# Position bias of an attention kernel: the activity tests on float16 whole distances, two of three on ScalarE, and the first sum out of PSUM in one VectorE instruction

## The chip, the core and the metric

The kernel runs on one core of a Trainium2 chip. Its five engines work side by side: TensorE (PE; its weight loads are PEld), VectorE (DVE), ScalarE (ACT), GpSimd (POOL) and SyncE (SP), which issues most of the DMAs. The metric is the time of one execution on the device in microseconds, lower is better.

## The reference

Attention with a learned position bias, then a three-way max block, then eight experts mixed by a doubly normalised gate. This case touches the position bias only:

```python
rel = (pos[:, None] - pos[None, :]).astype(np.float32)
psi_rel = np.log1p(np.abs(rel))
psi_i = np.log1p(np.maximum(pos[:, None].astype(np.float32), 1.0))
x = (psi_rel / psi_i)[..., None]
h = np.maximum(x @ w1 + b1, 0.0)      # 32 hidden units
bias = h @ w2                          # 8 heads
scores = scores + bias.transpose(2, 0, 1)[None, :, :, :]
```

There are 2 batches, 8 heads, 576 positions and a head width of 64. For a row i and a hidden unit d, the unit is active at column j where w1·log1p|i−j| + b1·log1p(i) is positive. The bias of a head is then a sum, over the active units, of w1·w2 (multiplied by log1p|i−j| / log1p(i)) and of b1·w2.

## The kernel before

The program has four stages one after the other: the position bias, which is written to a DRAM tensor `bias_d`; the attention of 8 heads; the max block; the experts. Each engine runs its instructions in the order in which the Python code issues them; nothing reorders them. An engine that waits holds up everything behind it in its own order.

The bias stage works in 36 steps (`g16`) of 16 rows i. A step needs four activity tiles (`gen_s(g)`, 144 in all), each [128, 576] in float16: 4 rows i times 32 hidden units on the partitions, 576 columns j along the row. They come from a table `lw` of float32 logarithms (L213, loaded in two parts and multiplied by w1 on ScalarE, L239): a test tile is a window of it, shifted by 4 columns from one `g` to the next. VectorE compares the window with a threshold (L282, giving +0.5 or −0.5) for 12 of every 20 tiles (`ON_DVE`), ScalarE takes the Sign of the window plus a bias (L280, giving +1 or −1) for the rest. The tiles lie in a pool of 12, three steps deep.

`bias_mm` (L323) multiplies each tile with 32-column weights on TensorE, in two float16 parts and two column halves, for two sums: `ps[0]` (A, to be multiplied by the logarithm) and `ps[1]` (B). That is 32 products a step. As the tests are ±, a constant has to be added: for B by two more products with `cb` (L332), for A by the bias of ScalarE's instruction.

`bias_ev` takes A out of PSUM: ScalarE scales it and adds the constant (L339), GpSimd multiplies the result by the table `l16` (L342, VectorE in the last two steps). `bias_out` (L347) takes B out of PSUM on VectorE, scales it and adds the first tile; the result `bo` goes to DRAM through SP's queue. VectorE's order within a step is: `gen_s` for the step after next, then `bo`. Two PSUM buffers for each sum let TensorE be one step ahead.

GpSimd also prepares the operands of the attention's first two heads (`prep_head`, by L61 for a copy that rounds, and L190 for the rest that the copy leaves): head 0 in 18 instructions, one after every second step, then head 1 in 12. Head 1's inputs are loaded in three parts in steps 9, 15 and 18.

Before the first test there is a chain on VectorE that makes the weights `wb` (L244 to L272). It starts when the parameters `par` have landed.

Of the kernel before, what the change touches and what calls it, by code (L numbers as in the profile page):

```python
# [27 lines left out]
SH = S // 2  # L28
# [22 lines left out]
def make_body(stop=None):  # L51
    def body(tc, a):
# [21 lines left out]
        with ctx, tc.manual_schedule():  # L74
# [16 lines left out]
            def prep_w64(r, hi, lo):  # L91
                """A float64 weight tile [128, 512], made float32 on its bits and split, in steps."""
# [4 lines left out]
                # the exponent's floor is where float32's lowest exponent, and so 0, is made  # L97
# [25 lines left out]
            def w_step(n=1, last=99):  # L123
                """The next n steps of the weights' preparation, up to an item."""
# [15 lines left out]
            # ------------------------------------------------ operands of the heads  # L140
# [25 lines left out]
            def prep_head(h, k, part=None):  # L166
                """Operands of head h, piece k: hi, then what is left."""
# [34 lines left out]
            # ------------------------------------------------ position bias  # L202
            with ExitStack() as bctx:
# [9 lines left out]
                cuts = (0, 476, L4_W)  # L213
                nc.scalar.dma_start(out=lw[:, cuts[1]:], in_=a["tab4"][:, cuts[1]:])
                dma(lw[:, :cuts[1]], a["tab4"][:, :cuts[1]])
# [5 lines left out]
                # products that nobody reads, to have the tensor engine's clock up when the data are there  # L221
# [6 lines left out]
                half = bc.tile([32, 96], F32, name="half")  # L228
                G.memset(half, 0.5)
                sel = bc.tile([96, SH], BF16, name="sel")  # L230
                G.memset(sel, 0.0)
                for p in range(3):
                    G.memset(sel[32 * p:32 * p + 1], 1.0)
                bcv = bc.tile([128, NG4], F32, name="bcv")
# [22 lines left out]
                # times 8, as the scores get their 1/8 with the bias in them  # L257
# [4 lines left out]
                # block-diagonal weights: [half-weights?, A or B, (i4, h)], in two float16 parts  # L262
                wf = bc.tile([128, 2, 2, 32], F32, name="wf")
                for q in range(2):
                    V.tensor_tensor(
                        out=wf[:, 0, q, :].rearrange("p (i h) -> p i h", h=H),
                        in0=ab[:, q, :].unsqueeze(1).to_broadcast([128, 4, H]),
                        in1=msk.rearrange("p (i h) -> p i h", h=H), op=ALU.mult)
                V.tensor_scalar(out=wf[:, 1], in0=wf[:, 0], scalar1=0.5, scalar2=None, op0=ALU.mult)
                wb = [bc.tile([128, 2, 2, 32], F16, name=f"wb{p}") for p in range(2)]  # L270
                V.tensor_copy(out=wb[0], in_=wf)
                V.tensor_tensor(out=wb[1], in0=wf, in1=wb[0], op=ALU.subtract)  # L272
                s_t = {}

                def gen_s(g):
                    s = sp.tile([128, S], F16, tag="s", name="s")
# [37 lines left out]
                def bias_mm(g16):  # L314
# [12 lines left out]
                    if g16 == 0:  # L327
                        consts()
                        for g in range(4, 8):
                            gen_s(g)  # L330
# [768 lines left out]
```

## Time and profile before

| what | us |
|---|---|
| median of 3 runs | 1179.74 |
| lowest and highest | 1177.23, 1180.08 |
| the profiled execution: span from the first to the last instruction (the page gives no other time of it) | 1179.2 |
| busy in the span: PE / DVE / ACT / POOL | 1130.2 / 744.1 / 513.9 / 381.2 |
| the bias stage: from the start to the end of the last `bo` (L347) | 115.2 |

The profile page holds the busy time of each engine, the span in 40 slices, the chain of work that ended last and the costliest groups of instructions. The shares of busy time are averages over four stages with different limits, so each stage is read by itself from a table of stretches and from the instructions in order of time. In such a row the first number is the start in us from the start of the span, the second the time in us, `x3` says that three like instructions in a row are merged, and a bracket gives idle time before the instruction and what ended it.

### The profile page before, as it was taken

Reading aid. Unit: us, or ns where it says so; the run is one execution under the profiler, and the core shown is the slowest. Engines: PE = TensorE matmul, PEld = TensorE weight load, DVE = VectorE, ACT = ScalarE, POOL = GpSimd, SP = SyncE. Lnnn points to the kernel's source line nnn. Section 1 sums busy time; section 2 is a strip of 40 time slices with the busy share of each in tenths; the row PEclk is TensorE's granted clock in tenths of the full one; section 3 lists DMA queues with packets and bytes.
Section 4 is the critical chain, followed back from the end, with each engine's and each line's share of the span. In section 5 each row is a group of like instructions: output and inputs, shape, how many; then the busy total and the mean of one; then the engine's idle time right before and its main releaser. Section 6 shows DMA issues by size and latency. Waiting matters only on the chain.

```text
span 1179.2 us, 19134 instructions
## 1 busy us (share of the span) xinstructions
PE 1130.2 (96%) x7654; PEld 1003.9 (85%) x7654; DVE 744.1 (63%) x1221; ACT 513.9 (44%) x884; POOL 381.2 (32%) x316
## 2 busy tenths in 40 slices
PE   7776999999999999999999999999999999999998
PEld 3333888999999988889989899899898998998987
DVE  8999999977774476746456365464463553644623
ACT  6665898863432463415225134153251341532510
POOL 5668578912220450513113022031131220321310
PEclk8889999999999999999999999999999999999999
DMA  4353666403330021102012021021120110211102
GB/s 152 132 185 124 215 202 213 140 30 108 108 113 31 19 73 35 45 28 72 27 46 65 17 64 45 28 72 34 39 72 9 63 45 28 73 36 36 55 18 81
DMA packets 35432, 87.77 MB, mean 74 GB/s; under 512 B 5455, under 2 KB 5774, under 8 KB 34446
## 3 DMA queue, kind: packets, MB, share of 16 engines
q1 hardware_dynamic: 35198, 86.20, 22.4%
q8 instruction: 60, 0.98, 0.3%
q10 hardware_dynamic: 144, 0.34, 0.1%
q14 instruction: 30, 0.25, 0.1%
HBM read 73.52 MB, written 13.01 MB: 73 GB/s over the span
## 4 chain that ended last, share of the span: by engine, by line
PE 72%; DVE 13%; issue 3%; ACT 2%; DMA 0%; DVEq 0%; ACTq 0%
PE d L1011 33%; PE x L929 12%; PE z L929 8%; PE y L929 8%; PE o L807 3%; PE m L581 3%; DVE ng L427 3%; DVE ptl L503 2%; DVE ww L100 1%; DVE ww L105 1%; PE sc L410 1%; DVE ww L103 1%; PE pv L540 1%; DVE x L553 1%; ACT ww L99 1%
## 5 line engine op out<-in xcount | busy, mean ns | idle before, releaser
L1022 DVE SCALAR_TENSOR_TENSOR acc<-d,P,acc 128x512 f32<-128x512 f32 x135 | 101.4, 751 | 239.8 <-PE d L1011 239.7
L997 POOL TENSOR_TENSOR w2l<-w2r,w2h 128x512 fp32r<-128x512 f32 x64 | 93.8, 1466 | 468.9 <-ACT w2h L996 445.9
L1011 PE MATMUL d<-w2h,hh 128*128 128x512 f32 x576 | 224.9, 390 | 0.0
L1011 PE MATMUL d<-w2h,hl 128*128 128x512 f32 x576 | 224.7, 390 | 0.0
L1011 PE MATMUL d<-w2l,hh 128*128 128x512 f32 x576 | 224.4, 390 | 0.0
L937 ACT ACTIVATE s<-x 128x576 f32<-128x576 f32 x96 | 62.5, 651 | 355.8 <-PE x L929 352.6
L942 ACT ACTIVATE hh<-s 128x576 fp32r<-128x576 f32 x128 | 87.9, 687 | 93.4 <-DVE s L954 43.4
L1011 PEld LDWEIGHTS d<-w2h,hl 128*128 128x128 f32 x576 | 108.1, 188 | 23.0 <-DVE hl L947 0.3
L1011 PEld LDWEIGHTS d<-w2l,hh 128*128 128x128 f32 x576 | 108.1, 188 | 22.0
L1011 PEld LDWEIGHTS d<-w2h,hh 128*128 128x128 f32 x576 | 108.2, 188 | 21.9
L947 DVE SCALAR_TENSOR_TENSOR hl<-s,hh 128x576 fp32r<-128x576 f32 x128 | 103.1, 823 | 1.8 <-ACT hh L942 1.5
L323 PE MATMUL p<-s,wb 128*32 128x288 f16 x1152 | 62.4, 325 | 25.2 <-DVE s L282 23.2
L929 PE MATMUL x<-xth,w1h 128*128 128x288 f32 x384 | 82.6, 297 | 0.5 <-ACT acc L810 0.5
L747 POOL TENSOR_TENSOR w1l<-wf,w1h 128x768 fp32r<-128x768 f32 x32 | 59.2, 1851 | 72.4 <-ACT w1h L746 72.4
L929 PE MATMUL x<-xtl,w1h 128*128 128x288 f32 x384 | 82.3, 296 | 0.0
L929 PE MATMUL x<-xth,w1l 128*128 128x288 f32 x384 | 82.1, 295 | 0.0
L323 PEld LDWEIGHTS <-wb 128*32 128x32 f16 x1152 | 32.8, 105 | 53.2 <-issue 37.8
L282 DVE TENSOR_SCALAR s<-lw,thr 128x576 f16<-128x576 f32 x86 | 76.3, 934 | 0.0
L581 PE MATMUL m<-xh,wh 128*128 128x384 f32 x216 | 73.8, 341 | 2.1 <-DVE t L699 2.0
L581 PE MATMUL m<-xl,wh 128*128 128x384 f32 x216 | 73.1, 338 | 0.0
L581 PE MATMUL m<-xh,wl 128*128 128x384 f32 x216 | 73.1, 338 | 0.0
L963 DVE TENSOR_TENSOR s<-y,s 128x576 f32<-128x576 f32 x32 | 24.2, 757 | 73.2 <-ACT w1h L750 68.4
(193 smaller groups left out, 2601.2 us busy)
## 6 DMA issues: line engine op xcount, KB each, us to landing
wf<-in_moe_w SPq DMA_DIRECT2D x32, 512.0 KB, 3.5
w2r<-in_moe_w SPq DMA_DIRECT2D x64, 256.0 KB, 2.5
bias_d<-bo SPq DMA_DIRECT2D x36, 288.0 KB, 2.2
bias<-bias_d SPq DMA_DIRECT2D x32, 288.0 KB, 3.0
wr<-in_moe_w SPq DMA_DIRECT2D x18, 512.0 KB, 3.4
qk<-in_qk SPq DMA_DIRECT2D x7, 1152.0 KB, 7.2
wr<-in_moe_w_out SPq DMA_DIRECT2D x6, 512.0 KB, 3.5
vr<-in_v SPq DMA_DIRECT2D x8, 320.0 KB, 5.0
```

Of the source, the lines that this page charges most:

```text
L282: V.tensor_scalar(out=s, in0=win, scalar1=thr[:, g:g + 1], scalar2=0.5, op0=ALU.is_gt, op1=ALU.subtract)
L323: T.matmul(out=pt[32 * c:32 * c + 32, hf, :SH], lhsT=wb[p][:, on_act, q, :], rhs=s[:, hf * SH:hf * SH + SH], start=(p == 0), stop=(p == 1 ...
L427: V.tensor_tensor_reduce(out=ng.rearrange("p (f n) -> p f n", f=2), in0=w["sc"][:, :, :SH], in1=bias_t[h, k // 2].rearrange("p (f n) -> p ...
L581: T.matmul(out=p[:, :TG], lhsT=ws[:, 128 * c:128 * c + 128], rhs=xs[:, c, TG * g:TG * g + TG], start=(c == 0 and n == 0), stop=(c == 3 and ...
L747: G.tensor_tensor(out=lo[:, 0:3], in0=t[:, 1:4], in1=raw(hi[:, 0:3]), op=ALU.subtract)
L929: T.matmul(out=ps[bank][:, s, :SH], lhsT=ws[:, i, c, :], rhs=xs[:, j, c, s * SH:s * SH + SH], start=(start and k == 0), stop=(k == 5), **kw)
L937: A.activation(out=t, in_=src, func=AF.Copy)
L942: A.activation(out=o, in_=src, func=AF.Relu)
L947: V.scalar_tensor_tensor(out=l, in0=src, scalar=0.0, in1=raw(o), op0=ALU.max, op1=ALU.subtract)
L997: G.tensor_tensor(out=lo, in0=r, in1=raw(hi), op=ALU.subtract)
L1011: T.matmul(out=pd, lhsT=hs[:, fh, 128 * t:128 * t + 128], rhs=ws, start=(k == 0), stop=(k == 11))
L1022: V.scalar_tensor_tensor(out=acc[:, t, :], in0=pd, scalar=P[:, t, e:e + 1], in1=acc[:, t, :], op0=ALU.mult, op1=ALU.add)
```

## The change

The tests no longer look at logarithms. The table becomes whole distances |i−j| in float16 (`rr`, one DMA on ScalarE's queue), multiplied once by the sign of w1 on VectorE (`rs`). The threshold becomes a distance: exp(−b1·log1p(i)/w1) − 1, worked out on VectorE by a polynomial on [128, 144] tiles. VectorE compares (result 0 or 1) for tiles 0 to 3 and every third one from tile 6, 50 in all (before: 86 on VectorE, 58 on ScalarE); ScalarE takes a steep Sigmoid of the other 94, against a rounded threshold plus one half. As the tests are 0 or 1, the constant parts, their products (L299, L300, L332) and their preparation on VectorE and GpSimd go. The first sum leaves PSUM in one VectorE instruction that scales it and multiplies it by `l16`; ScalarE's L339 and GpSimd's L342 go.

```diff
-ON_DVE = (0, 2, 4, 6, 8, 10, 11, 13, 14, 16, 18, 19)
+STEEP = 256.0
+def on_act(g):
+    return g > 3 and g % 3 > 0
...
-                lw = bc.tile([128, L4_W], F32, name="lw")
+                rr = bc.tile([128, L4_W], F16, name="rr")
...
-                nc.scalar.dma_start(out=lw[:, cuts[1]:], in_=a["tab4"][:, cuts[1]:])
-                dma(lw[:, :cuts[1]], a["tab4"][:, :cuts[1]])
+                nc.scalar.dma_start(out=rr, in_=a["tab4"])
...
-                pool_scale(bcv, c4, b1r)
-                pool_copy(thr, bcv, -1.0)
-                for sl in (slice(cuts[1], None), slice(0, cuts[1])):
-                    A.activation(out=lw[:, sl], in_=lw[:, sl], func=AF.Identity, scale=w1r)
+                ts(sg, w1r, 0.0, ALU.is_ge, 2.0, ALU.mult)
+                ts(sg, sg, -1.0, ALU.add)
+                ts(dn, w1r, sg, ALU.mult, 1e-30, ALU.max)
+                V.reciprocal(out=dn, in_=dn)
+                ts(kap, b1r, sg, ALU.mult, dn, ALU.mult)
+                ts(v, c4, kap, ALU.mult, -8.0, ALU.max)
+                ts(v, v, 8.0, ALU.min, -1.4426950408889634, ALU.mult)
+                ts(kf, v, MAGIC, ALU.add)
+                ts(kf, kf, -MAGIC, ALU.add)
+                V.tensor_tensor(out=f, in0=v, in1=kf, op=ALU.subtract)
+                ts(pw.bitcast(I32), kf, 127.0, ALU.add, 2.0 ** 23, ALU.mult)
+                taylor = [np.log(2.0) ** n / math.factorial(n) for n in range(8)]
+                ts(po, f, float(taylor[7]), ALU.mult)
+                for n in range(6, 0, -1):
+                    V.scalar_tensor_tensor(out=po, in0=po, scalar=float(taylor[n]), in1=f, op0=ALU.add, op1=ALU.mult)
+                V.scalar_tensor_tensor(out=po, in0=po, scalar=1.0, in1=pw, op0=ALU.add, op1=ALU.mult)
+                ts(thr, po, sg, ALU.mult, sg, ALU.subtract)
+                ts(rs, rr, sg, ALU.mult)
...
                 def gen_s(g):
                     s = sp.tile([128, S], F16, tag="s", name="s")
-                    win = lw[:, L4_OFF - 4 * g:L4_OFF - 4 * g + S]
-                    on_act = g % 20 not in ON_DVE
-                    if on_act:
-                        A.activation(out=s, in_=win, func=AF.Sign, bias=bcv[:, g:g + 1])
+                    win = rs[:, L4_OFF - 4 * g:L4_OFF - 4 * g + S]
+                    if on_act(g):
+                        A.activation(out=s, in_=win, func=AF.Sigmoid, bias=nthr[:, g:g + 1], scale=STEEP)
                     else:
-                        V.tensor_scalar(out=s, in0=win, scalar1=thr[:, g:g + 1], scalar2=0.5,
-                                        op0=ALU.is_gt, op1=ALU.subtract)
+                        V.tensor_scalar(out=s, in0=win, scalar1=thr[:, g:g + 1],
+                                        scalar2=None, op0=ALU.is_gt)
                 for g in range(4):
                     gen_s(g)
...
+                ts(po, po, -1.5, ALU.add, MAGIC, ALU.add)
+                ts(po, po, -MAGIC, ALU.add, 0.5, ALU.add)
+                ts(nthr, po, sg, ALU.mult, -STEEP, ALU.mult)
+                for g in range(4, 8):
+                    gen_s(g)
+                V.tensor_scalar(out=ics, in0=ic16, scalar1=sc[:, 1:2], scalar2=None, op0=ALU.mult)
...
-                    for hf in range(2):
-                        T.matmul(out=ps[1][:, hf, :SH], lhsT=cb, rhs=sel, start=False, stop=True)
                     return ps
...
                     t = ev.tile([128, S], F32, tag="t", name="t")
-                    A.activation(out=v3(t), in_=ps[0][:, :, :SH], func=AF.Identity, bias=ia0[:, g16:g16 + 1],
-                                 scale=ics[:, g16:g16 + 1])
-                    eng = G if g16 < NG16 - LASTV else V
-                    eng.tensor_tensor(out=t, in0=t, in1=l16[:, L16_OFF - 16 * g16:L16_OFF - 16 * g16 + S], op=ALU.mult)
+                    V.scalar_tensor_tensor(out=v3(t), in0=ps[0][:, :, :SH], scalar=ics[:, g16:g16 + 1],
+                                           in1=v3(l16[:, L16_OFF - 16 * g16:L16_OFF - 16 * g16 + S]),
+                                           op0=ALU.mult, op1=ALU.mult)
                     return t
```

VectorE before, from the last of the weights (`wb`) into the first step; `s` are test tiles, `aic`, `cb` and `cr` the constant parts, `bo` the finished rows:

```order
L272 TENSOR_TENSOR wb_171<-wf,wb_170 128x128
L282 TENSOR_SCALAR s<-lw,thr 128x576 x2
L303 TENSOR_SCALAR aic<-tab_113,sc 128x36
L304 COPY aic<-p_125 128x1
L305 TENSOR_SCALAR aic<-aic 128x36
L307 CAST cb<-p_125 96x128
L308 TENSOR_TENSOR cr<-p_125,cb 96x128
L310 CAST cb<-cr 32x128 x2
L311 TENSOR_TENSOR cr<-cr,cb 32x128
L312 CAST cb<-cr 32x128
L282 TENSOR_SCALAR s<-lw,thr 128x576 x5
L347 SCALAR_TENSOR_TENSOR bo<-p,sc,t 128x576
```

VectorE in the changed kernel, the same place; `eu` and `nthr` make ScalarE's thresholds, `ics` the scales of the first sum:

```order
L296 TENSOR_TENSOR wb_182<-wf,wb_181 128x64
L307 TENSOR_SCALAR s<-rs,thr 128x576 x4
L236 TENSOR_SCALAR eu<-eu 128x144 x2
L236 TENSOR_SCALAR nthr<-eu,one 128x144
L307 TENSOR_SCALAR s<-rs,thr 128x576
L319 TENSOR_SCALAR ics<-tab_113,sc 128x36
L339 SCALAR_TENSOR_TENSOR t<-p,ics,tab_113 128x576
L307 TENSOR_SCALAR s<-rs,thr 128x576
L346 SCALAR_TENSOR_TENSOR bo<-p,sc,t 128x576
```

Each step of VectorE now begins with `t` straight from PSUM (L339), and has one or two tests (L307) in the place of two or three.

GpSimd before, from its first thresholds to the first pieces of head 0 (`qs`, the queries):

```order
L64 TENSOR_SCALAR bcv<-par 128x144
L61 TENSOR_SCALAR thr<-bcv 128x144
L292 COPY ab_182<-ab 32x128 x2
L342 TENSOR_TENSOR t<-t,tab_113 128x576 x2
L61 TENSOR_SCALAR qs_76<-qk 128x576
L342 TENSOR_TENSOR t<-t,tab_113 128x576 x2
L190 TENSOR_TENSOR qs_76<-qk,qs_76 64x288
```

GpSimd in the changed kernel, from its last fill to the first pieces of head 0 (`kh` and `kl` are the keys):

```order
L154 MEMSET qs_79 128x64
L66 TENSOR_SCALAR qs_76<-qk 128x576
L195 TENSOR_TENSOR qs_76<-qk,qs_76 64x288 x2
L66 TENSOR_SCALAR qs_77<-qk 128x576
L195 TENSOR_TENSOR qs_77<-qk,qs_77 64x288 x2
L66 TENSOR_SCALAR kh_80<-qk 128x576
L195 TENSOR_TENSOR kl_84<-qk,kh_80 128x288 x2
```

Nothing stands between the pieces of a head any more: GpSimd can run them as soon as their inputs have landed.

ScalarE before, at the end of the bias stage (`pe` are the first exponentials of the attention):

```order
L280 ACTIVATE s<-lw,bcv 128x576 x2
L339 ACTIVATE t<-p,aic 128x576 x2
L99 ACTIVATE ww<-wr 128x512
L438 ACTIVATE pe,st<-ng,st 128x576 x2
L502 ACTIVATE pth_2054<-pt 128x4x128
```

ScalarE in the changed kernel, from its first instruction of the bias stage to the same place:

```order
L305 ACT_TABLE_LOAD
L305 ACTIVATE s<-rs,nthr 128x576 x94
L104 ACTIVATE ww<-wr 128x512
L437 ACT_TABLE_LOAD
L437 ACTIVATE pe,st<-ng,st 128x576 x2
L501 ACTIVATE pth_1945<-pt 128x4x128
```

Its stage is one run of tests, and two loads of a function table have come in.

## Rows read from the trace of the kernel before

**Rows 1.** The page, its first line.
```profile
span 1179.2 us, 19134 instructions
```

**Rows 2.** Table of stretches: PE, PEld, DVE, ACT, POOL busy; granted clock, DMA, GB/s.
```profile
90.00:110.00 20.00, 13.77 (x228) 6.74 (x229) 20.00 (x24) 11.42 (x17) 15.04 (x15) 0.91 0.31 111
```

**Rows 3.** Groups of instructions, 12 to 115.2 us: busy us, mean ns | idle before.
```profile
L282 DVE TENSOR_SCALAR s<-lw,thr 128x576 f16<-128x576 f32 x84 | 75.3, 944 | 0.0
...
L347 DVE SCALAR_TENSOR_TENSOR bo<-p,sc,t 128x576 f32<-128x576 f32 x36 | 29.0, 806 | 0.2
```

**Rows 4.** Instructions in order of time, VectorE, early steps.
```profile
17.90 4.28 DVE L282 TENSOR_SCALAR s<-lw,thr 128x576 f16<-128x576 f32 x3
22.10 0.80 DVE L347 SCALAR_TENSOR_TENSOR bo<-p,sc,t 128x576 f32<-128x576 f32 x1
22.83 0.93 DVE L282 TENSOR_SCALAR s<-lw,thr 128x576 f16<-128x576 f32 x2
23.68 0.80 DVE L347 SCALAR_TENSOR_TENSOR bo<-p,sc,t 128x576 f32<-128x576 f32 x1
```

**Rows 5.** Instructions in order of time, GpSimd, the same stretch and before it.
```profile
10.77 1.40 POOL L342 TENSOR_TENSOR t<-t,tab 128x576 f32<-128x576 f32 x1 [3.18 <-ACT t L339]
...
17.91 2.98 POOL L342 TENSOR_TENSOR t<-t,tab 128x576 f32<-128x576 f32 x2
20.97 0.89 POOL L190 TENSOR_TENSOR qs<-qk,qs 64x288 fp32r<-64x288 f32 x1
```

**Rows 6.** Instructions in order of time, VectorE, the start.
```profile
4.82 0.42 DVE L244 TENSOR_REDUCE big<-par 128x32 f32<-128x256 f32 x1 [3.43 <-DMA par<-in_par]
...
5.85 0.15 DVE L250 TENSOR_SCALAR big<-big 128x1 f32<-128x1 f32 x1
...
7.44 0.21 DVE L269 TENSOR_SCALAR wf<-wf 128x64 f32<-128x64 f32 x1
7.68 0.23 DVE L271 CAST wb<-wf 128x128 f16<-128x128 f32 x1
7.94 0.29 DVE L272 TENSOR_TENSOR wb<-wf,wb 128x128 f16<-128x128 f32 x1
8.15 0.94 DVE L282 TENSOR_SCALAR s<-lw,thr 128x576 f16<-128x576 f32 x2
...
10.93 1.31 DVE L312 CAST cb<-cr 32x128 bf16<-32x128 f32 x1
```

**Rows 7.** DMA issues of the first 12 us: KB each, us to landing.
```profile
qk<-in_qk SPq DMA_DIRECT2D x1, 1152.0 KB, 8.3
```

**Rows 8.** Groups of instructions, 12 to 115.2 us, GpSimd's halves of head 0's keys.
```profile
L190 POOL TENSOR_TENSOR kl<-qk,kh 128x288 fp32r<-128x288 f32 x4 | 4.0, 1009 | 0.0
```

**Rows 9.** Instructions in order of time, GpSimd, early attention: a piece's copy and rest.
```profile
125.27 0.67 POOL L61 TENSOR_SCALAR qs<-qk 128x576 fp32r<-128x576 f32 x1 [6.19 <-PE sc L410]
126.02 1.43 POOL L190 TENSOR_TENSOR qs<-qk,qs 64x576 fp32r<-64x576 f32 x1
```

**Rows 10.** Instructions in order of time, ScalarE, the start and the first exponential.
```profile
1.17 1.28 ACT L224 ACT_TABLE_LOAD   x1 [1.17 <-PEq L1089]
...
19.17 1.43 ACT L280 ACTIVATE s<-lw,bcv 128x576 f16<-128x576 f32 x2
...
115.92 0.78 ACT L438 ACTIVATE pe<-ng,st 128x576 f32<-128x576 f32 x1 [4.67 <-DVE st L427]
```

**Rows 11.** Instructions in order of time, VectorE, the end of the stage.
```profile
109.69 1.99 DVE L342 TENSOR_TENSOR t<-t,tab 128x576 f32<-128x576 f32 x1
...
114.39 0.82 DVE L347 SCALAR_TENSOR_TENSOR bo<-p,sc,t 128x576 f32<-128x576 f32 x1
```

**Rows 12.** Instructions in order of time, TensorE, two steps' products.
```profile
24.16 2.11 PE L323 MATMUL p<-s,wb 128*32 128x288 f16 x32
...
26.79 1.21 PE L323 MATMUL p<-s,wb 128*32 128x288 f16 x32
```

More of the change, by code (lines that the diff above doesn't have):

```diff
@@ L227, in body @@
                     T.matmul(out=p0[:, 1, :], lhsT=wz[:, :128], rhs=wz, start=True, stop=True)
[L228 to L234, printed above, removed]
-                thr = bc.tile([128, NG4], F32, name="thr")
@@ L236, in body, with ts @@
-                pool_scale(bcv, c4, b1r)
-                pool_copy(thr, bcv, -1.0)
-                for sl in (slice(cuts[1], None), slice(0, cuts[1])):
-                    A.activation(out=lw[:, sl], in_=lw[:, sl], func=AF.Identity, scale=w1r)
+                def ts(out, in0, s1, o0, s2=None, o1=None):
+                    kw = {} if o1 is None else {"op1": o1}
+                    V.tensor_scalar(out=out, in0=in0, scalar1=s1, scalar2=s2, op0=o0, **kw)
+                MAGIC = 1.5 * 2.0 ** 23
@@ new lines, in body @@
+                one = bc.tile([128, 4], F32, name="one")
+                sg, kap, dn = one[:, 0:1], one[:, 1:2], one[:, 2:3]
+                eu = bc.tile([128, 5, NG4], F32, name="eu")
+                v, kf, f, po, pw = (eu[:, i] for i in range(5))
+                thr = bc.tile([128, NG4], F32, name="thr")
+                nthr = bc.tile([128, NG4], F32, name="nthr")
+                rs = bc.tile([128, L4_W], F16, name="rs")
+                ts(sg, w1r, 0.0, ALU.is_ge, 2.0, ALU.mult)
+                ts(sg, sg, -1.0, ALU.add)
@@ L287, in body @@
                     gen_s(g)
-                ab16 = bc.tile([32, 2, 16, H], F32, name="ab16")
-                for q in range(2):
-                    G.tensor_copy(out=ab16[:, q], in_=ab[:32, q, :].unsqueeze(1).to_broadcast([32, 16, H]))
-                cb = bc.tile([96, 128], BF16, name="cb")
-                cr = bc.tile([96, 128], F32, name="cr")
-                aic = bc.tile([128, 1 + 2 * NG16], F32, name="aic")
-                a0, ia0, ics = aic[:, 0:1], aic[:, 1:1 + NG16], aic[:, 1 + NG16:]
@@ L298, in body @@
-                rows = ab16.rearrange("k q i h -> k q (i h)")
-                T.matmul(out=p0[:, 0, 0:1], lhsT=rows[:, 0], rhs=half[:, 0:1], start=True, stop=True)
-                T.matmul(out=p0[0:96, 0, 128:256], lhsT=half, rhs=rows[:, 1], start=True, stop=True)
-                def consts():
-                    V.tensor_scalar(out=ics, in0=ic16, scalar1=sc[:, 1:2], scalar2=None, op0=ALU.mult)
-                    V.tensor_copy(out=a0, in_=p0[:, 0, 0:1])
-                    V.tensor_scalar(out=ia0, in0=ics, scalar1=a0, scalar2=None, op0=ALU.mult)
-                    b0 = p0[0:96, 0, 128:256]
-                    V.tensor_copy(out=cb, in_=b0)
-                    V.tensor_tensor(out=cr, in0=b0, in1=cb, op=ALU.subtract)
-                    for p in (32, 64):
-                        V.tensor_copy(out=cb[p:p + 32], in_=cr[p:p + 32])
-                    V.tensor_tensor(out=cr[64:], in0=cr[64:], in1=cb[64:], op=ALU.subtract)
-                    V.tensor_copy(out=cb[64:], in_=cr[64:])
+                ts(po, po, -1.5, ALU.add, MAGIC, ALU.add)
@@ L321, in bias_mm @@
                                 for c in range(4):
-                                    s, on_act = s_t[4 * g16 + c]
-                                    T.matmul(out=pt[32 * c:32 * c + 32, hf, :SH], lhsT=wb[p][:, on_act, q, :],
-                                             rhs=s[:, hf * SH:hf * SH + SH], start=(p == 0), stop=(p == 1 and q == 0))
+                                    T.matmul(out=pt[32 * c:32 * c + 32, hf, :SH], lhsT=wb[p][:, q, :],
+                                             rhs=s_t[4 * g16 + c][:, hf * SH:hf * SH + SH], start=(p == 0), stop=(p == 1))
                     for c in range(4):
                         del s_t[4 * g16 + c]
[L327 to L330, printed above, removed]
-                    for hf in range(2):
-                        T.matmul(out=ps[1][:, hf, :SH], lhsT=cb, rhs=sel, start=False, stop=True)
                     return ps
```

14 lines of the change are left out of this document (7 added, 7 removed).

## The prediction

> **What bounds the kernel now.** I read the page's first line, then the table of stretches, the groups of the bias stage, and the instructions in order of time, VectorE beside GpSimd. The span is 1179.2 us [rows 1]; the median of the three runs is 1179.74, so 0.5 us are taken to lie around it, before and after alike. The bias stage ends with the last `bo`, at 114.39 + 0.82 = 115.2 us [rows 11], and the attention's first VectorE instruction follows at once. In the stretch from 90 to 110 us VectorE is busy for all of 20.00 us; no other engine is over 15.04 [rows 2]. So VectorE sets the length of this stage, and what it saves there shortens the program.
>
> What does it do in that time? A `bo` costs 0.73 us from its start to the next instruction's (22.10 to 22.83). Two tests in a quiet moment cost 0.85 (22.83 to 23.68), 0.43 each [rows 4]. Yet the mean test takes 944 ns, and 84 of them are 75.3 us of the 103 us [rows 3]. The difference is GpSimd: three tests from 17.90 took 4.28 us, while GpSimd ran two multiplications in 2.98 and a subtraction in 0.89 [rows 4, 5]. Each test ended shortly after one GpSimd instruction had. A test that comes while GpSimd works waits until that instruction is over, and GpSimd's next one follows it. `bo`, which reads PSUM and one SBUF tile, takes 806 ns in the mean of 36 and 0.80 in quiet [rows 3, 4]: it does not wait. A VectorE product of two SBUF tiles does: 1.99 us for `t` at 109.69 [rows 11]. A small conversion did too, 1.31 at 10.93, behind the multiplication from 10.77 [rows 5, 6].
>
> **The change, part by part.** I follow VectorE to the end of the last `bo`.
>
> *Start.* `par` lands at 4.82 [rows 6], as now: its DMA stays first in SP's queue. Then 21 new instructions come ahead of the weights' chain. Five are on one column: 0.15 and a gap of 0.04 each, 0.95 together. Seven with one input on 144 columns: one on 64 columns takes 0.24 to its follower (7.44 to 7.68), I take 0.27, so 1.9. Eight with two inputs: 0.29 for 128 columns (7.94) and the gap, 0.33, so 2.6 [rows 6]. `rs` on 1148 columns lies between one test and two, 0.43 to 0.86; I take 0.6. That is 6.1. The weights' chain took 8.15 − 4.82 = 3.33 and loses one instruction of 0.24: 3.1.
>
> Then come four tests, three instructions for ScalarE's thresholds, a fifth test and `ics`. A test from float16 to float16 does not occur in the trace. Above, it is bounded by the same test from float32, 0.43; below, by an instruction with few columns, 0.24 [rows 4, 6]. I take the middle, 0.33, since the shape is the row's and half the bytes are read. 5 × 0.33 + 4 × 0.27 = 2.7. The first `t` could start at 4.8 + 6.1 + 3.1 + 2.7 = 16.7. TensorE's first 16 products fit beside the thresholds.
>
> *The collision at the start.* Before, head 0's 18 pieces on GpSimd were spread over the stage, one behind every second step. Now nothing stands ahead of them but the landing of `qk`, issued at 2.1 and landed 8.3 later, at 10.4 [rows 7]; with 0.3 MB less in front of it, about 9.7. So GpSimd runs them back to back just when VectorE still has some 22 instructions before the first `t` that have two SBUF inputs, or one and an SBUF output, in short ones of 0.2 to 0.6 us. If none waits, this costs 0. If each of the 18 pieces is waited for whole, 18 × 0.85 (a mean of pieces between 0.67 and 1.01 [rows 8, 9]) = 15. I take 8: many of the pieces will be waited for, but the chain also holds three reductions and single-column work beside which GpSimd gets on. First `t`: 24.7.
>
> *The steps.* ScalarE's and GpSimd's way for the first sum goes; VectorE gets `t`, with the operands of `bo` (PSUM, one SBUF tile, a column), so 0.73. 36 × 2 × 0.73 = 52.6. Left are 45 tests × 0.33 = 14.9. Together 67.4, or 1.87 a step. A new wait stands at the head of each step: `t` waits for TensorE's first 16 products, and behind it on VectorE are the tests of two steps on and `bo`. TensorE is a step ahead (two PSUM buffers, 12 tiles): its 32 products take 1.2 us at the high clock [rows 12], inside 1.87, so I price the wait at nothing. If that cover goes, it is a rival below.
>
> *Head 1.* Its 12 pieces come when its inputs do, after steps 9, 15 and 18: four copies of 0.67 and four rests of 1.4 [rows 9], and four shorter ones, about 11 us of GpSimd in all, against a test every 1.4 us. Waiting costs 0 to 11; I take 4. After that GpSimd is idle to the end of the stage, where the two `t` at 109.69 and later also lose their waits (their price is already in the new `t`).
>
> *ScalarE.* 94 tests at 0.67 (two in 1.43, which overlap by 0.1 [rows 10]) from 24.1 end at 87.0; eight products, `t` and `bo` make it 89.1. It is close, but not last. Two table loads come in; one took 1.28. The first lies in ScalarE's idle start, the second where ScalarE now waits 4.67 for the first maximum [rows 10]; both cost nothing. If that idle time is gone, the second costs 1.3.
>
> *Sum.* 16.7 + 8 + 67.4 + 4 = 96.1 in the place of 115.2: 19.1 less. The attention finds the same engines in the same state, so the rest keeps its length. 1179.7 − 19.1 = 1160.6.
>
> Two sentences of the Trainium skill beside this. VectorE: DVE Perf Modes (The perf-mode tier table) gives a single-input instruction on 16-bit data twice the rate of float32; by it a test would be an estimated 0.28 and the sum 2 us less, 1158; no run here shows such a test. SBUF — State Buffer (Who interferes with whom) says the fast modes for 16-bit data lock GpSimd out, and are locked out, just as those of float32 are, and that one SBUF input beside PSUM is free of it; the trace agrees for float32 (4.28 against 0.93) and for `bo`, and by this rule the change keeps collisions that the smaller data might be thought to end.
>
> **The rivals.**
>
> *No collisions (1149).* The short instructions slip between GpSimd's, or float16 tests don't wait: 16.7 + 67.4 = 84.1, 31.1 less, 1148.6. ScalarE would then allow 16.1 + 62.9 + 2.1 = 81.1. For it: the chain's instructions are short, and smaller data may leave room. Against: the one short instruction of the start that met GpSimd, at 10.93, waited for all of it [rows 5, 6].
>
> *Collisions in full and no faster test (1174).* A test stays at 0.43, 12 us are lost at the start and 8 with head 1: 17.2 (five tests at 0.1 more) + 12 + 52.6 + 19.4 + 8 = 109.2, 6 less. For it: every float32 test that met GpSimd waited.
>
> *TensorE takes over (1164).* At the low clock 32 products took 2.11, at the high one 1.21 [rows 12]; the granted clock was 0.91 in the stretch, so it does fall at times. If it stayed low, 36 × 2.1 = 75.6 in the place of 67.4 and 4: about 4 more than forecast. Against: two products fewer per step and a steadier feed.
>
> *Slower (1217).* ScalarE's Sigmoid costs more than its Sign, say twice: 1.34 each, 24.1 + 94 × 1.34 + 2.1 = 152.2, 37 more. It decides from 0.95 us a test, where ScalarE's run would end at 115.2. Against: an exponential of the same shape takes 0.78 [rows 10], as Sign does.
>
> *No change.* Both collisions at their ends with the slow test, and `rs` at 0.86, give 17.5 + 15 + 52.6 + 19.4 + 11 = 115.5: nothing gained.
>
> **How the numbers follow.** Forecast 0.53, no collisions 0.22, collisions in full 0.13, TensorE 0.07, slower 0.03, no change 0.02. A measurement here tells 0.3% (3.5 us) from no change. All of the first four are faster by more: 0.95; same 0.02; slower 0.03. The low end of all terms is 1145 (a test at 0.24 and `rs` at 0.43, no collisions: VectorE ends at 16.0 + 52.6 + 10.8 = 79.4, ScalarE last at 15.4 + 62.9 + 2.1 = 80.4), the high end 1180. The forecast's own range is 1153 to 1168. For 8 in 10 I take most of the first rival and leave out the upper part of the second: 1147 to 1170.
>
> **What would show it.** Right: the last `bo` ends near 96; `t` and `bo` at 0.8 each, never longer; VectorE busy without gaps; the first `t` near 25, with short instructions of 0.6 to 1.1 us among the chain from 10 us on, each ending after a GpSimd piece; tests under 0.43 (start to start) after 60 us; GpSimd's head 0 done before 30; ScalarE's run ending 5 us or more before VectorE's; from the first maximum on, the same distances as now. Wrong: a first `t` near 17 (first rival), idle time of VectorE before `t` put down to TensorE or to ScalarE's tiles, a Sigmoid over 0.8, a table load in front of the first exponential with VectorE waiting, or an attention that is longer than now.

## The result, and the profile of the changed kernel

The changed kernel takes 1157.66 us (median of 4 runs, 1157.55 to 1158.34) against 1179.38 for the kernel before (4 runs, 1177.23 to 1180.08). The ratio is 0.9822, with an interval from 0.9808 to 0.9835: 21.7 us faster, where 19.1 were forecast.

The page of the changed kernel begins as follows; the counterpart of the span is in [rows 1].

```profile
span 1156.2 us, 18994 instructions
PE 1111.5 (96%) x7578; PEld 1000.2 (87%) x7578; DVE 722.4 (62%) x1234; ACT 509.5 (44%) x884; POOL 324.9 (28%) x273
```

Next, two stretches of its bias stage and the first 10 us of its attention: length, then busy time and number of instructions of PE, PEld, DVE, ACT and POOL, then the granted clock, the DMA share and GB/s. They answer to [rows 2].

```profile
12.00:22.00 10.00, 3.49 (x33) 1.74 (x34) 9.52 (x26) 1.45 (x3) 9.43 (x15) 0.50 0.00 0
30.00:50.00 20.00, 15.72 (x375) 10.60 (x377) 20.00 (x36) 20.00 (x31) 2.09 (x2) 1.00 0.60 206
89.80:99.80 10.00, 9.59 (x60) 8.77 (x59) 8.32 (x20) 7.73 (x19) 0.02 (x1) 0.83 0.81 282
```

VectorE still has no idle time in the steps, but now ScalarE has none either from 30 to 50 (20.00 us each). The start is where VectorE and GpSimd are busy side by side. The groups of the stage (out<-in, shapes, count, busy us and mean ns, idle time before and its releasers) answer to [rows 3]:

```profile
L305 ACT ACTIVATE s<-rs,nthr 128x576 f16<-128x576 f16 x94 | 63.2, 762 | 17.0 <-DVE nthr L236 16.5 <-PE p L329 0.4
L346 DVE SCALAR_TENSOR_TENSOR bo<-p,sc,t 128x576 f32<-128x576 f32 x36 | 29.1, 807 | 0.2
L339 DVE SCALAR_TENSOR_TENSOR t<-p,ics,tab 128x576 f32<-128x576 f32 x36 | 29.0, 804 | 0.1
L307 DVE TENSOR_SCALAR s<-rs,thr 128x576 f16<-128x576 f16 x50 | 21.1, 445 | 0.0
```

The tests of VectorE went from 75.3 us to 21.1, and `t` came in with 29.0, at the price of a `bo`. VectorE in order of time, at the landing of `par`, at the start's collision, in the first two steps, under head 1's pieces, and at the end of the stage (answering to [rows 4, 6, 11]):

```profile
4.43 0.15 DVE L236 TENSOR_SCALAR one<-par 128x1 f32<-128x1 f32 x1 [3.03 <-DMA par<-in_par]
...
15.65 0.72 DVE L295 CAST wb<-wf 128x64 f16<-128x64 f32 x1
16.41 0.62 DVE L296 TENSOR_TENSOR wb<-wf,wb 128x64 f16<-128x64 f32 x1
16.95 2.47 DVE L307 TENSOR_SCALAR s<-rs,thr 128x576 f16<-128x576 f16 x4
...
21.69 0.82 DVE L339 SCALAR_TENSOR_TENSOR t<-p,ics,tab 128x576 f32<-128x576 f32 x1
22.43 0.36 DVE L307 TENSOR_SCALAR s<-rs,thr 128x576 f16<-128x576 f16 x1
22.70 0.81 DVE L346 SCALAR_TENSOR_TENSOR bo<-p,sc,t 128x576 f32<-128x576 f32 x1
...
60.60 0.77 DVE L307 TENSOR_SCALAR s<-rs,thr 128x576 f16<-128x576 f16 x1
...
88.94 0.82 DVE L346 SCALAR_TENSOR_TENSOR bo<-p,sc,t 128x576 f32<-128x576 f32 x1
89.80 0.76 DVE L426 CUSTOM_DVE_ANT_0 ng<-sc,bias 128x576 f32<-128x576 f32 x1
```

A quiet test, one with no GpSimd piece beside it, takes 0.27 us from its start to its follower's (22.43 to 22.70); four at 16.95 took 2.47, and the one at 60.60 took 0.69 to its follower at 61.29. GpSimd at those times (answering to [rows 5, 9]):

```profile
8.79 0.75 POOL L66 TENSOR_SCALAR qs<-qk 128x576 fp32r<-128x576 f32 x1 [7.14 <-DMA qk<-in_qk]
...
17.04 1.73 POOL L195 TENSOR_TENSOR kl<-qk,kh 128x288 fp32r<-128x288 f32 x2
...
20.93 1.00 POOL L195 TENSOR_TENSOR vs<-vr,vs 128x192 fp32r<-128x192 f32 x2
...
60.54 0.67 POOL L66 TENSOR_SCALAR kh<-qk 128x576 fp32r<-128x576 f32 x1
```

Head 0 is prepared in one go from 8.79 to 21.93, and the first `t` comes at its end. The test from 60.60 meets the copy that started at 60.54: the copy ends at 61.21, the test at 61.37. ScalarE's tests and its table load (answering to [rows 10]):

```profile
20.55 46.74 ACT L305 ACTIVATE s<-rs,nthr 128x576 f16<-128x576 f16 x70 [16.48 <-DVE nthr L236]
...
84.81 1.28 ACT L437 ACT_TABLE_LOAD   x1
90.60 0.78 ACT L437 ACTIVATE pe<-ng,st 128x576 f32<-128x576 f32 x1 [4.51 <-DVE st L426]
```

70 tests in 46.74 us are 0.668 each. The table load added ahead of the exponential stands in idle time: the first exponential still waits 4.51 us behind it, for VectorE.

**Where the time came from.** The stage's last `bo` ends at 89.76, before at 115.21 [rows 11]: 25.4 us earlier. The spans differ by only 23.0 and the medians by 21.7; what became of the other 3.7 is taken up by repeats of both kernels, below.

### The profile page after: what moved, and what is told of

The parts are those of the page before. It is cut to its first block, busy times and chain, and to the rows that moved or that the text cites. A ratio compares the mean times of both kernels' runs of the same rounds, so it can differ in the third digit from the quotient of the medians.

```text
span 1156.2 us, 18994 instructions
## 1 busy us (share of the span) xinstructions
PE 1111.5 (96%) x7578; PEld 1000.2 (87%) x7578; DVE 722.4 (62%) x1234; ACT 509.5 (44%) x884; POOL 324.9 (28%) x273
## 4 chain that ended last, share of the span: by engine, by line
PE 69%; DVE 16%; issue 4%; ACT 3%; DMA 1%; DVEq 0%; ACTq 0%; SPq 0%
PE d L1010 34%; PE x L928 11%; PE y L928 8%; PE z L928 7%; PE o L806 3%; DVE ng L426 3%; DVE ptl L502 2%; PE m L580 2%; DVE ww L108 1%; DVE ww L105 1%; DVE ww L110 1%; PE pv L539 1%; DVE pth L502 1%; PE sc L409 1%; DVE x L552 1%
## 5 line engine op out<-in xcount | busy, mean ns | idle before, releaser
L329 PE MATMUL p<-s,wb 128*32 128x288 f16 x1152 | 56.6, 292 | 24.5 <-DVE s L307 15.7
L305 ACT ACTIVATE s<-rs,nthr 128x576 f16<-128x576 f16 x94 | 63.2, 762 | 17.0 <-DVE nthr L236 16.5
```

The lines of the kernel that those rows point to most:

```text
L305: A.activation(out=s, in_=win, func=AF.Sigmoid, bias=nthr[:, g:g + 1], scale=STEEP)
L329: T.matmul(out=pt[32 * c:32 * c + 32, hf, :SH], lhsT=wb[p][:, q, :], rhs=s_t[4 * g16 + c][:, hf * SH:hf * SH + SH], start=(p == 0), stop=( ...
```

## The experiments

Two theories stood against each other on the part that the trace of before could not show, the collision with GpSimd. By the one it costs VectorE some 8 us in the changed kernel (5 at the start and 3 with head 1) and can be taken out; by the other the start and the steps are bound by something else. Besides, each part of the change was undone alone: the first sum, the format, the split of the tests, the function on ScalarE. Ratios are against runs of the kernel before on the same chip: median 1178.20 (9 runs) for the first four told here, 1178.63 (7 runs) for the float32 tests, the old split and the last version. Where spans, starts or ends are named, they are those of the profiled execution.

**GpSimd held back until the first step.**

```diff
+                gt = bc.tile([128, 1], F16, name="gt")
...
+                    if g16 == 0:
+                        G.tensor_copy(out=gt, in_=s_t[11][:, 0:1])
                     if g16 % 2:
```

> GpSimd's first piece of head 0 is held back until VectorE has made its test of step 0 (one small GpSimd copy that reads a column of that test tile); all else as in the changed kernel. Theory A (short VectorE instructions wait for whole GpSimd pieces): the first t starts at 16 to 17 us in the place of 21.7, as 5 us of the start are waiting; the 18 pieces then meet some ten tests in the steps and cost 2 to 4 there, so the last bo ends at 87 to 89 (89.8 now) and the time falls by 1 to 3 us. Rival B (the start is late because the chain is long, and GpSimd costs it nothing): the first t stays at 21 to 22 and the time within 0.5 us.

1154.04 us (1152.47 to 1154.77), ratio 0.9798 (0.9780 to 0.9815). One thing in the expectation is wrong: tile 11 is made by ScalarE, so GpSimd waited for ScalarE's last tile of step 0, and started at 19.78 rather than behind a test of VectorE's. VectorE, and GpSimd behind it:

```profile
13.38 1.20 DVE L308 TENSOR_SCALAR s<-rs,thr 128x576 f16<-128x576 f16 x4
...
15.88 0.82 DVE L340 SCALAR_TENSOR_TENSOR t<-p,ics,tab 128x576 f32<-128x576 f32 x1
...
18.67 0.82 DVE L340 SCALAR_TENSOR_TENSOR t<-p,ics,tab 128x576 f32<-128x576 f32 x1 [0.97 <-PE p L330]
...
21.41 0.36 DVE L308 TENSOR_SCALAR s<-rs,thr 128x576 f16<-128x576 f16 x1
...
23.14 0.36 DVE L308 TENSOR_SCALAR s<-rs,thr 128x576 f16<-128x576 f16 x1
...
84.06 0.82 DVE L347 SCALAR_TENSOR_TENSOR bo<-p,sc,t 128x576 f32<-128x576 f32 x1
```

```profile
19.52 0.28 POOL L365 COPY gt<-s 128x1 f16<-128x1 f16 x1 [17.87 <-ACT s L306]
...
20.65 1.77 POOL L195 TENSOR_TENSOR qs<-qk,qs 64x288 fp32r<-64x288 f32 x2
22.52 0.67 POOL L66 TENSOR_SCALAR qs<-qk 128x576 fp32r<-128x576 f32 x1
```

The first `t` starts at 15.88 and not at 21.69: the collision at the start is 5.8 us, and the four tests that took 2.47 take 1.20. The stage ends 4.9 earlier, at 84.88, more than the 1 to 3 that were expected, for head 0's pieces, which had to go somewhere, cost almost nothing among the steps: the tests at 21.41 and 23.14 are as short as a quiet one. Two pieces of 0.67 to 0.80 fit, one behind the other, into the 1.46 us in which VectorE does `bo` and `t`. A GpSimd piece that meets a test waits for it (the copy at 25.01 beside two tests took 1.03 us, at 22.52 0.67), and from then on runs beside the two instructions that do not collide. Whole pieces of head 1, 0.67 + 1.42, don't fit, and six tests beside them took 0.48 to 0.88. By the medians the time falls by 3.6 us, a little more than expected too.

**Every GpSimd piece put behind a test.** 34 pieces, one a step, each behind the step's last test by VectorE, head 1's longer rests in halves:

```diff
+                pieces = [lambda k=k, p=p: prep_head(0, k, p) for k in (0, 2, 4, 6, 7, 8) for p in range(3)]
+                pieces += [lambda k=k, p=p: prep_head(1, k, p) for k in (0, 2, 4, 6) for p in range(3)]
+                pieces += [lambda k=k, p=p: prep_head(1, k, p) for k in (7, 8) for p in (0, 3)]
...
-                    if g16 % 2:
-                        prep_head(0, (0, 2, 4, 6, 7, 8)[g16 // 6], g16 // 2 % 3)
+                    if g16 < NG16 - 2:
+                        G.tensor_copy(out=gt, in_=s_t[max(g for g in range(4 * g16 + 8, 4 * g16 + 12) if not on_act(g))][:, 0:1])
+                        pieces[g16]()
...
-                    if s < NU and k in PREP and h + 1 < H:
+                    if s < NU and k in PREP and 1 < h + 1 < H:
```

> Each of 34 GpSimd pieces (head 0 in 18, head 1 in 16) is held back until VectorE has made the last test of one step, one piece a step, so that it runs beside bo and the next t. Theory A: no collision is left, neither at the start (5.3 us) nor with head 1 (about 3): first t at 16 to 17, every test at 0.28 from start to start, last bo at 81 to 83, time 1149 to 1151. Rival B (GpSimd costs little): last bo over 87, time over 1155. If ScalarE is then last, its run of 94 tests ends within 2 us of the last bo.

1148.70 us (1148.03 to 1150.15), ratio 0.9756 (0.9739 to 0.9772). VectorE's rows, with GpSimd's behind the test at 43.05 below:

```profile
15.74 0.82 DVE L340 SCALAR_TENSOR_TENSOR t<-p,ics,tab 128x576 f32<-128x576 f32 x1
...
18.44 0.82 DVE L340 SCALAR_TENSOR_TENSOR t<-p,ics,tab 128x576 f32<-128x576 f32 x1 [0.87 <-PE p L330]
...
43.05 0.35 DVE L308 TENSOR_SCALAR s<-rs,thr 128x576 f16<-128x576 f16 x1
...
81.11 0.82 DVE L347 SCALAR_TENSOR_TENSOR bo<-p,sc,t 128x576 f32<-128x576 f32 x1
```

```profile
43.54 0.19 POOL L369 COPY gt<-s 128x1 f16<-128x1 f16 x1 [0.99 <-DVE s L308]
43.68 0.45 POOL L195 TENSOR_TENSOR vs<-vr,vs 128x128 fp32r<-128x128 f32 x1
```

GpSimd does its work in the pause between two tests. All 50 tests come at 0.276, the stage ends at 81.93: 7.8 before the changed kernel, and the time falls by 9.0. The first `t` and the time come out a little under the expected 16 to 17 and 1149 to 1151. So the theory of the collisions holds for its place and its size: the first `t` comes 5.95 earlier, and from there to the end of the stage it is 1.9 less, in which VectorE also waits 0.87 for TensorE at the second `t`; head 1's pieces had thus cost 2.75. The tests say the same: from start to follower the 50 sum to 18.2 us in the changed kernel, 16.6 with only head 0 held back, 13.9 here.

**The old way of the first sum**, with the new tests (`zero` is a column of zeros):

```diff
...
-                    V.scalar_tensor_tensor(out=v3(t), in0=ps[0][:, :, :SH], scalar=ics[:, g16:g16 + 1],
-                                           in1=v3(l16[:, L16_OFF - 16 * g16:L16_OFF - 16 * g16 + S]),
-                                           op0=ALU.mult, op1=ALU.mult)
+                    A.activation(out=v3(t), in_=ps[0][:, :, :SH], func=AF.Identity, bias=zero,
+                                 scale=ics[:, g16:g16 + 1])
+                    G.tensor_tensor(out=t, in0=t, in1=l16[:, L16_OFF - 16 * g16:L16_OFF - 16 * g16 + S], op=ALU.mult)
```

> The first sum leaves PSUM on ScalarE again and is multiplied by the table on GpSimd; the float16 tests and their new split stay. Theory A (the one VectorE instruction takes work off ScalarE, and GpSimd's part away): a step becomes ScalarE's 2.67 x 0.667 + 0.73 = 2.5 us, 36 of them 90, last bo at 110 to 116, time 20 to 27 us over the changed kernel. Rival (the gain is the cheaper test alone, and the way of the first sum is indifferent): at most 8 us over it.

1172.73 us (6 runs, 1171.65 to 1173.78), ratio 0.9958 (0.9945 to 0.9971).

```profile
30.00:50.00 20.00, 14.07 (x257) 7.86 (x257) 12.27 (x19) 20.00 (x30) 14.42 (x13) 1.00 0.42 150
```

```profile
42.37 0.82 DVE L348 SCALAR_TENSOR_TENSOR bo<-p,sc,t 128x576 f32<-128x576 f32 x1 [1.56 <-POOL t L343]
...
106.34 0.82 DVE L348 SCALAR_TENSOR_TENSOR bo<-p,sc,t 128x576 f32<-128x576 f32 x1 [0.56 <-POOL t L343]
```

ScalarE has no pause and VectorE waits for it through GpSimd: the bound has moved to ScalarE, as expected, and the stage ends at 107.16. The size was over, +15.1 instead of 20 to 27. A full step takes 2.49, as expected, but the last two have no tests, and ScalarE begins earlier than I had taken, at 15.59 and not at 20.55: with the multiplications between them head 0's pieces are spread over the stage again, and the collision at the start is gone. The +15.1 is thus what remains after that gain. Without the one-instruction first sum the change is worth a quarter of what it is worth with it.

**Sign in the place of the Sigmoid**, so that no table load is added; ScalarE's tiles are then −1 or 1 instead of 0 or 1.

```diff
-                        A.activation(out=s, in_=win, func=AF.Sigmoid, bias=nthr[:, g:g + 1], scale=STEEP)
+                        A.activation(out=s, in_=win, func=AF.Sign, bias=nthr[:, g:g + 1], scale=STEEP)
```

> ScalarE takes Sign in the place of Sigmoid, which leaves out the two added table loads; its tiles hold +1 and -1 where 0 and 1 are wanted. Theory A (the loads lie in idle time): the time within 0.5 us, last bo at 89.8 within 0.5. Rival (a load stands in front of the first exponential, or Sigmoid is dearer than Sign): 1.3 us or more faster.

1158.16 us (1156.76 to 1159.55), ratio 0.9834 (0.9816 to 0.9853): no difference that can be measured from the changed kernel's 0.9822.

```profile
20.58 41.41 ACT L305 ACTIVATE s<-rs,nthr 128x576 f16<-128x576 f16 x62 [17.81 <-DVE nthr L236]
```

```profile
90.33 0.82 DVE L346 SCALAR_TENSOR_TENSOR bo<-p,sc,t 128x576 f32<-128x576 f32 x1
```

62 tests in 41.41 us are 0.668 each: the Sigmoid costs no more than Sign, and its table loads cost nothing that shows in the time. The stage missed its expectation, 89.8 within 0.5: it ends at 91.15. In this execution GpSimd's pieces meet the tests otherwise (the 50 sum to 19.9 us and not 18.2), and the second `t` waits 0.56 us for TensorE; whether that comes from the edit or from the execution was not tried.

**The tests from float32** (the table `rs` alone in float32):

```diff
-                rs = bc.tile([128, L4_W], F16, name="rs")
+                rs = bc.tile([128, L4_W], F32, name="rs")
```

> VectorE's and ScalarE's tests read the whole distances from a float32 copy of the table (rs) in the place of the float16 one; all else as in the changed kernel. Theory A (VectorE ends the stage, and the float16 test is worth 0.43 - 0.28 = 0.15 us): 45 tests after the first t cost 7 us more, last bo at 96 to 99 (89.8 now), time 6 to 9 us over the changed kernel. Rival (ScalarE, busy throughout too, sets the pace, and the cheaper test is hidden): at most 2 us over it.

1164.37 us (1164.19 to 1164.66), ratio 0.9881 (0.9867 to 0.9896).

```profile
73.06 0.50 DVE L307 TENSOR_SCALAR s<-rs,thr 128x576 f16<-128x576 f32 x1
73.49 0.80 DVE L346 SCALAR_TENSOR_TENSOR bo<-p,sc,t 128x576 f32<-128x576 f32 x1
...
96.82 0.82 DVE L346 SCALAR_TENSOR_TENSOR bo<-p,sc,t 128x576 f32<-128x576 f32 x1
```

A quiet test takes 0.43, as before; the 50 of them sum to 25.1 us and not 18.2, the first `t` comes 1.0 later, and the stage ends at 97.64, 7.9 later. In the time float16 is worth 6.7 us.

**The old split of the tests** (12 of 20 on VectorE, 88 in all):

```diff
-    return g > 3 and g % 3 > 0
+    return g > 3 and g % 20 not in (0, 2, 4, 6, 8, 10, 11, 13, 14, 16, 18, 19)
```

> Twelve of twenty tests on VectorE as before the change (after the first four), with the new tests and the new first sum. Theory A: a step of VectorE is 2 x 0.73 + 2.4 x 0.28 = 2.13 us, 36 of them 76.6 in the place of 66, and more tests meet head 1's pieces: last bo at 100 to 104, time 10 to 14 us over the changed kernel. Rival (two of three on ScalarE is not needed, the gain is the removal of GpSimd's multiplications): at most 4 us over it.

1166.83 us (1166.11 to 1170.25), ratio 0.9900 (0.9883 to 0.9916): +9.2, a little under the expected 10 to 14. The stage ends at 102.60, inside the 100 to 104: 12.8 later, which is about what the 88 tests take more than the 50 (30.8 us and 18.2).

```profile
101.78 0.82 DVE L346 SCALAR_TENSOR_TENSOR bo<-p,sc,t 128x576 f32<-128x576 f32 x1
```

This stage is that of the profiled execution, 1170.25 us, the longest of the four: 11.9 over the changed kernel's profiled one. The other three took 1166.11 to 1166.96, and where they were shorter is not shown.

**Both kernels once more**, four executions of the kernel before and one of the changed one, each with its profile, for the 3.7 us between the stage's gain and that of the medians.

> The kernel before, profiled once more, to see how far its bias stage and the rest vary by themselves. The bias stage ended 25.4 us earlier in the profile of the changed kernel, and the medians are 21.7 apart. If that is the spread of single executions, this one's stage (115.2 then) or its rest (1064.0 then) differs by 1 to 3 us; if the changed kernel's later stages are really longer, both stay within 0.5.

> The kernel before again, one profiled execution of three. The stage gained 25.4 us and the medians 21.7. Theory A (the stage of before is steady): its last bo ends at 115.1 to 115.5 whatever the span is, and a span of 1174 to 1177 has a rest (first maximum to the end) of 1059 to 1062, 4 us under the 1066 of the changed kernel; then some 4 us are given back behind the stage. Theory B (the two profiles of before caught long executions of the stage): in an execution with a span of 1174 to 1177 the last bo ends at 111 to 114, and the rest is 1063 to 1066 as in the changed kernel.

> As for the other executions of the kernel before: by theory A the last bo ends at 115.1 to 115.5 and the rest varies with the span; by theory B the end of the last bo varies with the span and the rest is 1063 to 1066.

> As for the other executions of the kernel before: by theory A the last bo ends at 115.1 to 115.5 and the rest varies with the span; by theory B the end of the last bo varies with the span and the rest is 1063 to 1066.

> The changed kernel again, one profiled execution. Theory A (its longer rest belongs to it): the last bo ends at 89.5 to 90.0, the rest is 1065.5 to 1067, and the stretch of low clock behind the 16 small products comes again. Theory B (its rest was that of one execution): the rest falls to 1062 to 1064, and that stretch is gone or elsewhere.

With the first profiles, in us (the rest is the time from the first maximum, `ng`, the attention's first VectorE instruction, to the end of the span):

```
                 time      span      last bo ends   rest
before           -         1179.17   115.21         1064.04
before, again    1180.04   1178.26   115.36         1062.98
before, again    1179.67   1177.89   115.23         1062.74
before, again    1181.90   1180.11   115.34         1064.85
before, again    1180.12   1178.35   114.67         1063.76
changed          1158.34   1156.20    89.76         1066.40
changed, again   1156.51   1154.56    90.09         1063.90
```

The stage is 25.2 us shorter in the mean and scatters by 0.7 at most; the spans are 23.4 apart, so 1.8 are lost behind the stage: 0.4 between the last `bo` and the first maximum, 0.2 from there to the first of VectorE's sums over the experts (`acc`), and 1.2 among these sums. A part of this is scatter. The 0.4 come mostly from the changed kernel's second execution, where the first maximum waits 0.57 us for TensorE. The stretch of low clock at the end of the attention, some 0.8 us in the changed kernel, is gone in its second execution and there in two of the kernel before; it follows 16 products of nine rows. Three stretches of 8 us at the same place of the program show it (1.00 is 2.4 GHz all the time; 0.79 means that 3.4 of the 8 us ran at 1.2 GHz): the changed kernel, its second execution, and the third execution of before in the table (columns as above):

```profile
228.00:236.00 8.00, 8.00 (x45) 7.70 (x44) 4.83 (x9) 2.52 (x5) 1.28 (x1) 0.79 0.19 62
```

```profile
228.00:236.00 8.00, 8.00 (x55) 7.60 (x54) 5.15 (x10) 2.77 (x6) 1.29 (x1) 1.00 0.20 65
```

```profile
252.00:260.00 8.00, 8.00 (x46) 7.69 (x45) 4.74 (x9) 2.71 (x6) 1.28 (x1) 0.79 0.19 60
```

Another part is not scatter. The 135 sums over the experts come in a rhythm: nine of them take 46.91 us, nearly everywhere. The fourth group of nine takes 46.91 in all five executions of the kernel before and 47.33 to 47.61 in all nine profiles with the new tests; the tenth takes 46.91 in all five and 47.15 to 47.47 in six of the nine. At the first of these places VectorE's remainder of a weight waits for its load and then stands beside GpSimd; VectorE and GpSimd in the changed kernel, then VectorE in the kernel before:

```profile
660.12 1.20 DVE L737 TENSOR_TENSOR wf<-wf 128x256 f32<-128x256 f32 x1 [0.74 <-DMA wf<-in_moe_w]
```

```profile
659.75 1.29 POOL L996 TENSOR_TENSOR w2l<-w2r,w2h 128x512 fp32r<-128x512 f32 x1 [1.66 <-ACT w2h L995]
```

```profile
684.12 0.41 DVE L738 TENSOR_TENSOR wf<-wf 128x256 f32<-128x256 f32 x1
```

So theory B of the last expectation holds for the low clock and for the rest, which fell to 1063.90; A holds only for the two places in the experts, 0.95 and 0.90 us together in the changed kernel's two executions. The seventh and the ninth group are scatter: 0.85 us longer together in the changed kernel's first profile, 0.80 in one of the kernel before, and 46.91 each in the others of this table. Why the load is waited for at the first of the two places, while everything of that expert's code is the same, was not tried.

The theories on the kernel before can't be told apart: no profiled execution fell into the spans of 1174 to 1177 that they speak of. In the first repeat the rest was 1.06 shorter and the stage as long as before, which speaks for a spread of the rest. All four repeats took 1179.67 to 1181.90, while the 21 other executions on record took 1175.42 to 1180.08; the changed kernel's two in the table lie on both sides of its median. The last 1.7 us, from 23.4 in the profiled spans to 21.7 in the medians, thus stay unexplained.

**ScalarE makes the exponential**, on top of the pieces behind the tests, with its own thresholds ahead of VectorE's first tests. Thirteen VectorE instructions go:

```diff
-                ts(v, v, 8.0, ALU.min, -1.4426950408889634, ALU.mult)
...
-                V.scalar_tensor_tensor(out=po, in0=po, scalar=1.0, in1=pw, op0=ALU.add, op1=ALU.mult)
-                ts(thr, po, sg, ALU.mult, sg, ALU.subtract)
-                ts(rs, rr, sg, ALU.mult)
+                V.tensor_scalar(out=v, in0=v, scalar1=8.0, scalar2=None, op0=ALU.min)
+                A.activation(out=rs, in_=rr, func=AF.Copy, scale=sg)
+                A.activation(out=po, in_=v, func=AF.Exp, scale=-1.0)
...
+                ts(thr, po, sg, ALU.mult, sg, ALU.subtract)
```

> As the run with every GpSimd piece held back, and the start shortened: ScalarE makes the exponential and the table with w1's sign (12 VectorE instructions and one go), and ScalarE's thresholds come before the first four tests. Theory A (VectorE is the chain from the landing of the parameters to the last bo): 12 instructions of 0.24 to 0.34 and the table's 0.43 go, the first t at 11.9 to 13 (15.7 there), last bo at 77.5 to 79 (81.9 there), time 1144 to 1146. Rival (ScalarE's run of 94 tests is last, or TensorE's low clock at the start): last bo over 80, time over 1147.

1141.30 us (1140.65 to 1142.75), ratio 0.9687 (0.9672 to 0.9701): 37.3 us under the kernel before, and 16 under the changed one. It beats both. VectorE, and the first 10 us of the attention:

```profile
12.31 0.82 DVE L332 SCALAR_TENSOR_TENSOR t<-p,ics,tab 128x576 f32<-128x576 f32 x1 [0.78 <-PE p L322]
...
76.88 0.82 DVE L339 SCALAR_TENSOR_TENSOR bo<-p,sc,t 128x576 f32<-128x576 f32 x1
```

```profile
77.70:87.70 10.00, 9.24 (x67) 7.86 (x65) 9.26 (x24) 8.69 (x21) 0.29 (x1) 1.00 0.79 277
```

The first `t` at 12.31 now waits 0.78 us for TensorE, so VectorE's chain is no longer all that holds it. The stage ends at 77.70, as expected. The time is 3 us under the lower end of the expected 1144 to 1146, and this lies behind the stage: 1061.12 from the first maximum on, the shortest of all. A part has a place: at the attention's start the granted clock is 1.00 here (2.4 GHz throughout) and 0.83 in the changed kernel (the last row of the stretches above; 3.4 us at 1.2 GHz), and the fifth maximum follows the first by 4.14 us here and by 5.13 there. TensorE had stood idle for 1.66 us before the attention's first product here, for 1.78 there. Why the clock did not fall here was not tried.

## Why the prediction was right, and where its terms were off

*The bound and the path.* That VectorE sets the stage's length, and that the attention begins when it is done, held: in six of the nine profiles with the new tests the first maximum comes within 0.1 us of the end of the last `bo` (in the other three it waits 0.57 for TensorE), and each run that took time from VectorE took it from the total, as long as VectorE was the bound.

*Start (16.7, measured 15.9).* The first `t` without a collision starts at 15.88 and 15.74 in the two runs that hold GpSimd back. Of the 0.8 to 1.0 less, 0.3 and 0.5 are the landing of `par`, at 4.49 and 4.35 and not at 4.82; the five tests are 0.25 and the weights' chain 0.2. The new chain was priced rightly from rows of few columns, 6.0 for 6.1.

*The collision at the start (8, measured 5.8).* Right in kind: short instructions from 9.7 on stretch to 0.6 to 0.9 us, while the reductions and most of those on one column do not (the one at 11.67 took 0.41 us with GpSimd and without). Too high by 2.2: of the 13.1 us that head 0 takes VectorE lost 44%, where 8 would have been 61%. The rival without collisions was wrong, as was the one with 12.

*A test (0.33, measured 0.276).* 45 × 0.054 = 2.4 less. I took the middle between a row of more bytes and one of few columns; the value lies near the lower one. The rate that VectorE: DVE Perf Modes (The perf-mode tier table) of the Trainium skill gives for 16-bit data had led to an estimated 0.28, and the trace agrees. That such tests still wait for GpSimd (0.62 each at 16.95, 0.69 at 60.60, against 0.276) is what SBUF — State Buffer (Who interferes with whom) of the Trainium skill says; the trace agrees here too. All collisions together, float32 and float16, cost the stage 8.6 us.

*`t` and `bo` (0.73 each).* Measured 0.73; means 804 and 807 ns, never longer beside GpSimd.

*Head 1 (4, measured 2.75).* Of 11 us of GpSimd a quarter was waited for. Its pieces ran on to 65.5 us, so the sign that tests take under 0.43 came from there on and not from 60.

*ScalarE and the table loads.* 0.668 a test for 0.67, its run ends at 84.20 for 87.0; the loads cost nothing that shows. But it is closer to the bound than it seemed: where VectorE doesn't wait, as from 30 to 50 us, both have no pause. The old first sum on ScalarE would have made it the bound, and this is why moving that sum to VectorE and the tests to ScalarE belong together.

*TensorE.* The granted clock was 1.00 (2.4 GHz) from 30 to 90 us; that rival was wrong, as were the slow Sigmoid and no change.

*The sum.* 96.1 for the end of the stage, measured 89.8: 0.8 at the start, 2.2 and 1.25 of collisions and 2.1 of the steps without them (67.4, measured 65.3) make up the difference of 6.3. All four errors have the same sign.

*The rest keeps its length.* This step failed, by the 0.9 us that the runs show at two places in the experts, and by 1.8 in the mean of the profiled executions, of which the other half is in part scatter. That 1157.7 came out as near 1160.6 as it did is thus in part a cancellation, and so luck: the stage gained 6.3 more than forecast, and 3.7 of it are not in the medians. The time around the span, taken as 0.5, is 1.8 to 2.1 in all runs that list both; by that the first profiled execution of the kernel before took an estimated 1181 us (1179.17 + 1.8) and not its median of 1179.7, which the 0.5 had hidden.

## What to carry to other kernels

A collision between VectorE and GpSimd is a matter of phase: put GpSimd's pieces behind the last colliding instruction of a step, cut to the length of the stretch that reads PSUM, and the same work costs VectorE nothing (it had cost 5.8 and 2.75 us here). Moving a sum out of PSUM into one VectorE instruction pays if VectorE is given something back, here float16 tests and two of three tests on ScalarE; undone one at a time, the sum, the format and the split cost 15.1, 6.7 and 9.2 us. What stands behind a changed stage may lengthen by a microsecond although its code is the same (0.9 us here, at one place with a load that is waited for; the cause is open): compare several executions before it is put down to chance or to the change.

## What the runs showed of the hardware that was not expected

- GpSimd pieces of 0.67 to 0.80 us fall into step with VectorE by themselves once a test has held one up, and then cost nothing: 0.36 us for the tests at 21.41 and 23.14, beside GpSimd's from 20.65 and 22.52.
- A compare of 576 float16 columns against a column threshold takes 0.276 us to its follower, from float32 0.43; a Sigmoid of the same tile on ScalarE 0.668, and a Sign as much.
- The same 8 us at the end of the attention run at a granted clock of 0.79 in one execution and of 1.00 in the next of the same kernel.
- The four repeats of the kernel before took 1179.67 to 1181.90 us, its 21 other executions 1175.42 to 1180.08; why was not tried.
